# Attention with two mixture layers behind it: six of nine token blocks of the first layer moved behind the attention

## The chip, the core and the metric

The program runs on one core of a Trainium2 chip. The metric is the device time of one execution in microseconds; of the kernel before there are three runs, 1027.32, 1027.60 and 1028.91 us, median 1027.60. Names of engines: PE multiplies matrices (PEld loads its weights), DVE and ACT do elementwise work, POOL next to nothing here, SP issues the transfers.

## What is computed

Three layers in a row, in float32. B = 4, H = 8 heads, S = 576 positions, D = 64; 2304 tokens of 512 values; both feed-forward layers are 512 to 2048 to 512.

```python
scores = scale * np.matmul(q, k.transpose(0, 1, 3, 2))
scores = np.where(causal, -1000000000.0, scores)
a = np.exp(scores - scores.max(-1, keepdims=True))
a /= a.sum(-1, keepdims=True) + 1e-09
local = np.matmul(a, v)
q_p = phi(q)                                  # phi(x) = elu(x) + 1
mem_out = (q_p @ M_prev) / (q_p . z_prev + 1e-06)
attn = g * mem_out + (1 - g) * local          # g = sigmoid(beta)
x = attn as [2304, 512]
h = x @ w_in;  x = (h * sigmoid(h)) @ w_out   # "MoE 1"
h = x @ w2_in; x = elu(h) @ w2_out            # "MoE 2"
```

## The kernel before

**The planner.** The kernel's functions don't issue instructions. They record operations in a list (`Plan.add`), each with an engine, a cost and what it reads and writes. `Plan.schedule` (L301) then places them on the engines by a list scheduler with a cost model, forward and backward in turns, and `Plan.order` (L273) gives the sequence in which they are issued. So every engine works through a fixed queue, and all instructions carry the line of one helper, L192. A `boost` raises the rank of the first eight attention tasks, `nc.ahead(n)` that of what stands inside it.

**Attention** (`attention`, L963). A task is one pair of heads and a region of queries: "A" is queries 0 to 255, "B" 256 to 575, each with the keys up to its diagonal. Batch 0 has A and B as tasks of their own, the others one task for both, 20 tasks in all. `soft` (L762) makes the scores on PE, then on DVE the masked, negated scores with their minimum (`e<-s,mask`, in the trace CUSTOM_DVE_ANT_0), then on ACT the exponential with its row sum, on DVE the reciprocal of the sum times the gate (`sm<-sm,og`, RECIPROCAL), and the scaled weights, on ACT for the tiles "2", "3" and "4", on DVE for the "A" tiles. Each exponent tile `e` has one buffer per head and kind, so a task's minimum must wait until PE has transposed the task before (`a_T`, `b_T`: `tp<-ident,e`). `mem_soft` and `mem_T` make the memory term. `av_mm` and `av_end` (L890) multiply by the values; the last matmul of a region is `av<-pt,ms`, which closes it: 32 of these, called attention ends below. The result is copied to a tile `xt` and stored in `xdA`/`xdB`.

**Precision.** A float32 matrix is split into a high and a low part (`split2`, L428: a cast on ACT, a subtraction on DVE), and each product of two of them is three matmuls. The weights of MoE 1 and MoE 2 come as float64 and are taken apart by `w_value` (L488): a scaling on ACT, a TENSOR_SCALAR and two SCALAR_TENSOR_TENSOR on DVE for each tile; with `w_split` after it, ACT has two instructions for a tile and DVE four. 32 such tiles make MoE 1 (`w_stream`, L506), streamed beside the attention.

**MoE 1.** Nine token blocks of 256: (b, "A") and (b, "B") for four batches, and "T", the last 64 tokens of each batch. `moe1_block` (L560) does one block with 256 columns a matmul, 16 steps f of 12 matmuls for the first product (`h<-x,w`) and 12 for the second (`acc<-g,w`), that is 384 matmuls; between them ACT makes the tanh (`t<-h`), DVE `t<-t,h`, ACT and DVE the two parts of `g`. `moe1_wide` (L642) does two blocks together with 512 columns, 384 matmuls for both, with tiles in the pool `p2`, whose memory is that of the attention's pool `at`: nothing in `p2` may start before the last user of `at` is done. `first` (L1057) lists the blocks that go 256 wide beside the attention: 0A and 0B in two halves, then 1A, 1B and 2A (`LAST = 5`); `interleave` (L985) sets in which measure they are recorded between the attention's steps. Behind it come the wide pairs (3A, 3B) and (2B, T) (L1321, L1335).

**MoE 2** runs behind that, with its weights prepared from the second wide pair on.

Of the kernel before, what the change touches and what calls it, by code (L numbers as in the profile page):

```python
# [21 lines left out]
NORM = '234'  # L22
NATN = '234'
# [3 lines left out]
LAST = 5  # L27
# [3 lines left out]
PASSES = 4  # L31
COLD = 0.3735
NFILL = 70
LEND = 4
NAG = 1
LATE = 60
NAT1 = []
NAT2 = []
# [5 lines left out]

BOOST = 1000.0
# [107 lines left out]
class Plan:  # L153
# [147 lines left out]
    def schedule(self, back):  # L301
# [26 lines left out]
        for _ in ops:  # L328
# [5 lines left out]
            o = ops[heapq.heappop(ready[e])[1]]  # L334
# [26 lines left out]
def attention_moe_moe_kernel(  # L361
# [71 lines left out]
    mask = new(const, [128, 768], BF16, "mask")  # L433
# [9 lines left out]
    for p0, rows, c0, n in ((0, 128, 384, 128), (0, 64, 704, 64), (64, 64, 704, 64)):  # L443
# [26 lines left out]
    again = []  # L470

    whole = [(c, 2 * j + u) for c, js in ((0, NAT1), (1, NAT2)) for j in js for u in range(2)]

# [14 lines left out]
    def w_value(raw):  # L488
# [6 lines left out]
        nc.vector.scalar_tensor_tensor(out=raw[:, 0:512], in0=hi_w, scalar=3, in1=lo_w,  # L495
# [5 lines left out]
    def w_split(f, c, v):  # L501
        t = w_tile(f, c)
        split2(t[:, 512:1024], t[:, 0:512], v)
        (win, wout)[c][f] = t

    def w_stream(srcs, ahead, place, whole=(), last=2 * NF):  # L506
        todo = [(f, c) for f in range(NF) for c in range(2)]
        raws = {}

        def fetch(k):  # L510
            if k < len(todo) and k not in raws:
                f, c = todo[k]
                raws[k] = w_load(srcs[c], f, c, w_tile(f, c, I32) if (c, f) in whole else place(k))
# [4 lines left out]
        for k, (f, c) in enumerate(todo):  # L518
            fetch(k)
            raw = raws.pop(k)  # L520
            w_value(raw)
            if (c, f) in whole:
                (win, wout)[c][f] = raw
            else:
                w_split(f, c, f32(raw[:, 0:512]))
            if k + ahead < last:
                fetch(k + ahead)
            yield

    def w_again(c, f):  # L530

        v = new(mp, [128, 512], F32, "t", 2)
        nc.scalar.copy(v[:], f32((win, wout)[c][f][:, 0:512]))
        w_split(f, c, v[:])
# [25 lines left out]
    def moe1_block(blk, half, xraw, wnext=None, mid=None):  # L560
        j0, j1 = {None: (0, NF // 2), 0: (0, JH), 1: (JH, NF // 2)}[half]
        nat = (NAT1, NAT2) if half is not None else ((), ())
# [12 lines left out]
        def gemm1(j):  # L575
            for _ in range(NAG):
                if again:
                    w_again(*again.pop(0))
            hb = bank("h", 1)
            h = hb[:].rearrange("p (a n) -> p a n", a=2)  # L580
            if j not in nat[0] and not xt:
                x_split()
            for u in range(2):
                w = win[2 * j + u]
                n = 0
                for kt in range(4):
                    c = slice(kt * 128, (kt + 1) * 128)
                    if j in nat[0]:
                        mm(h[:, u, :], f32(w[:, c]), xraw[:, kt, :], kt == 0, kt == 3)
                        yield  # L590
                        continue
# [5 lines left out]
            g = None if j in nat[1] else new(mp, [128, 2, 2, 256], F32R, "g", 2)  # L597
            g_t[j] = g or t
            with nc.ahead(HP):
                nc.scalar.activation(t[:], h, AF.Tanh, scale=0.5)  # L600
                nc.vector.scalar_tensor_tensor(out=t[:], in0=t[:], scalar=1.0, in1=h, op0=ALU.add, op1=ALU.mult)
                if g:
                    split(g, t[:])

        def gemm2(j):
            g = g_t.pop(j)
            for u in range(2):
                w = wout[2 * j + u]
                for dm in range(4):
# [3 lines left out]
                    if j in nat[1]:  # L613
                        mm(acc[dm // 2][:, dm % 2, :], f32(w[:, c]), g[:, u, :], s0, last)
                        yield
                        continue
# [76 lines left out]
    bet = new(at, [128, H], F32, "sm40", 2)  # L693
    gg = new(at, [128, H], F32, "sm230", 2)
# [15 lines left out]
    def load(task):  # L710
# [14 lines left out]
        z = new(at, [128, 128], F32, "zb", 2)  # L725
# [36 lines left out]
    def soft(task, nms):  # L762
# [3 lines left out]
        tiles = [[], []]  # L766
        heads = range(1 if nms == "4" else 2)
        small = [new(at, [128, 8], F32, f"sm{nms}{u}", 2) for u in heads]
        for nm in nms:
            e = [new(at, [128, wide[nm]], F32, f"e{nm}{u}") for u in heads]  # L770
            for u in heads:
                e_t[task, u, nm] = e[u]
            if nm == "4":
                for i in range(2):
                    s = bank("s", 2)
                    c, n = ((0, 320), (320, 256))[i]
                    scores(task, [s[0:64, 0:n], s[64:128, 0:n]], 512, 576, c, c + n)
                    masked(e[0][:, c:c + n], s[:, 0:n], (0, 512)[i], 3e38 if i == 0 else small[0][:, 0:1],
                           small[0][:, i:i + 1])
                tiles[0].append((e[0], 0, 576, 1))  # L780
                continue
            s = [bank("s", 2), bank(f"acc{p % 2}") if rg == "A" else bank("s", 2)]
            parts = [(0, 0, 128), (1, 128, 256)] if nm == "A" else [(int(nm), 0, wide[nm])]
            for qt, off, n in parts:
                scores(task, [s[u][:, off:off + n] for u in heads], qt * 128, qt * 128 + 128, 0, n)
            for u in heads:
                for qt, off, n in parts:
                    c = len(tiles[u])
                    masked(e[u][:, off:off + n], s[u][:, off:off + n], 512 - n, 3e38, small[u][:, c:c + 1])
                    tiles[u].append((e[u], off, n, c))  # L790
        for u in heads:
            sm = small[u]
            for i, (e, off, n, c) in enumerate(tiles[u]):
                nc.scalar.activation(e[:, off:off + n], e[:, off:off + n], AF.Exp, scale=-1.0,
                                     bias=sm[:, c:c + 1], accum_out=sm[:, 2 + i:3 + i])
            k = len(tiles[u])
            r = sm[:, 4:4 + k]
            h = 2 * p + u
            nc.vector.tensor_scalar(out=r, in0=sm[:, 2:2 + k], scalar1=1e-9,
                                    scalar2=op[:, p:p + 1] if nms == "4" else og[:, h:h + 1], op0=ALU.add, op1=ALU.mult)  # L800
            nc.vector.reciprocal(out=r, in_=r)
            for i, (e, off, n, c) in enumerate(tiles[u]):
# [615 lines left out]
```

## Time and profile before

| | |
|---|---|
| runs | 1027.32, 1027.60, 1028.91 us |
| profiled execution | 1026.67 us, of it the span from first to last instruction 1024.5 us |
| PE busy | 1007.5 us (98%), 6534 matmuls |
| PEld busy | 848.9 us (83%) |
| DVE busy | 686.3 us (67%) |
| ACT busy | 599.4 us (59%) |
| transfers | 98.00 MB, mean 96 GB/s |
| granted TensorE clock, mean | 0.997 |

The page shows the busy share in 40 slices of 25.6 us as well: PE is at 7 tenths in the first two slices and at 9 or more behind them, DVE and ACT are high in the first seven and lower afterwards. A busy share is a mean over stages that have different limits, so the rows below are cut by stage. PE's busy time is that of overlapping, modelled spans (a 256-column matmul is shown as some 280 ns long and the next one starts 120 ns after it), so that the price of a matmul is read from start to start. The 2.2 us between 1024.5 and 1026.67 lie outside the instructions.

### The profile page before, as it was taken

What the parts mean: (1) busy time and instruction counts of PE and PEld (TensorE: products, weight loads), DVE (VectorE), ACT (ScalarE), POOL (GpSimd) and SP (SyncE); (2) the same over time, 40 slices, a digit from 0 to 9 for tenths busy, and PEclk for the clock granted to TensorE, in tenths of its full rate; (3) what the DMA queues carried; (4) which work ended last, traced back from release to release, by engine and by line L of the source; (5) the groups of instructions that cost most, each with busy time, mean ns of one, the idle gap of its engine ahead of it and who ended that gap; (6) DMA issues with size and microseconds to landing.
All of it is one profiled execution on the core that took longest, in us unless ns stands there. A gap on an engine that the chain in (4) does not pass through costs nothing.

```text
span 1024.5 us, 17493 instructions
## 1 busy us (share of the span) xinstructions
PE 1007.5 (98%) x6534; PEld 848.9 (83%) x6534; DVE 686.3 (67%) x1734; ACT 599.4 (59%) x1374; POOL 6.2 (1%) x30
## 2 busy tenths in 40 slices
PE   7799999999999999999999999999999999999998
PEld 5366877778777779998888888999899998989987
DVE  7999998656556553622223587969679975656554
ACT  6899998767667764423224455656567554444433
POOL 1000000000000000000000000000000000000000
PEclk9899999999999999999999999999999999999999
DMA  8655844333222212301003135323226130302010
GB/s 254 215 182 171 251 147 146 95 94 101 76 64 81 88 38 84 101 1 42 1 1 96 47 125 164 93 93 124 83 83 201 47 124 1 123 1 93 11 62 21
DMA packets 96724, 98.00 MB, mean 96 GB/s; under 512 B 10880, under 2 KB 82048, under 8 KB 96640
## 3 DMA queue, kind: packets, MB, share of 16 engines
q1 hardware_dynamic: 96640, 96.89, 30.3%
q8 instruction: 51, 0.84, 0.3%
q14 instruction: 33, 0.27, 0.1%
HBM read 76.94 MB, written 19.92 MB: 95 GB/s over the span
## 4 chain that ended last, share of the span: by engine, by line
PE 94%; DVE 2%; ACT 2%; DMA 1%; issue 0%; SPq 0%; DVEq 0%; ACTq 0%
PE acc L192 26%; PE s L192 19%; PE h L192 18%; PE tp L192 17%; PE av L192 13%; ACT e L192 1%; DVE w L192 1%; DMA raw<-in_moe_w_in 0%; DVE e L192 0%; SPq L192 0%; DVE eA L192 0%; DMA k<-in_kT 0%; ACT a L192 0%; ACT w L192 0%; ACT eA L192 0%
## 5 line engine op out<-in xcount | busy, mean ns | idle before, releaser
L192 PE MATMUL acc<-g,w 128*128 128x256 f32 (+1 forms) x1152 | 194.2, 310 | 0.0
L192 PEld LDWEIGHTS acc<-g,w 128*128 128x128 f32 x1152 | 161.5, 190 | 18.2 <-issue 9.2
L192 PE MATMUL s<-x,w 128*128 128x256 f32 (+1 forms) x1056 | 173.7, 302 | 0.0
L192 PEld LDWEIGHTS s<-x,w 128*128 128x128 f32 x1056 | 155.6, 190 | 14.1
L192 PE MATMUL h<-x,w 128*128 128x256 f32 x960 | 142.6, 293 | 0.1
L192 PE MATMUL tp<-x,w 128*128 128x256 f32 (+1 forms) x864 | 141.2, 306 | 0.0
L192 PEld LDWEIGHTS h<-x,w 128*128 128x128 f32 x960 | 124.2, 190 | 11.3 <-issue 8.7
L192 PEld LDWEIGHTS tp<-x,w 128*128 128x128 f32 x864 | 124.2, 190 | 9.6
L192 PE MATMUL acc<-w,g 128*128 128x512 f32 x480 | 127.9, 392 | 0.0
L192 ACT ACTIVATE e<-e,sm 128x384 f32<-128x384 f32 (+2 forms) x160 | 104.8, 687 | 7.3 <-DVE sm L192 7.2
L192 PEld LDWEIGHTS acc<-w,g 128*128 128x128 f32 x480 | 86.4, 189 | 14.4
L192 ACT COPY a<-tp 128x384 f32<-128x384 f32 (+2 forms) x160 | 64.2, 425 | 35.2 <-PE tp L192 30.3
L192 DVE SCALAR_TENSOR_TENSOR w<-w 128x512 int32<-128x512 int32 x116 | 78.3, 687 | 1.7 <-ACT w L192 0.4
L192 PE MATMUL s<-k,q 64*128 64x384 f32 (+5 forms) x368 | 71.0, 465 | 5.1 <-DMA k<-in_kT 3.1
L192 DVE CUSTOM_DVE_ANT_0 e<-s,mask 128x384 f32<-128x384 f32 (+2 forms) x80 | 45.3, 594 | 31.3 <-PE tp L192 29.9
L192 ACT CAST g<-e 128x512 fp32r<-128x512 f32 (+1 forms) x80 | 46.0, 578 | 34.1 <-DVE e L192 33.9
L192 DVE TENSOR_TENSOR g<-t,g 128x512 fp32r<-128x512 f32 x72 | 49.6, 688 | 23.6 <-ACT g L192 23.4
L192 ACT ACTIVATE e<-h 128x512 f32<-128x512 f32 (+1 forms) x80 | 47.0, 590 | 31.4 <-DVE h L192 30.6
L192 DVE TENSOR_TENSOR g<-e,g 128x512 fp32r<-128x512 f32 (+1 forms) x80 | 50.6, 635 | 21.6 <-ACT g L192 20.5
L192 PE MATMUL tp<-ident,e 128*128 128x128 f32 (+1 forms) x304 | 59.8, 284 | 3.4 <-ACT e L192 1.9
L192 ACT CAST g<-t 128x512 fp32r<-128x512 f32 x72 | 44.8, 622 | 26.3 <-DVE t L192 25.3
L192 DVE SCALAR_TENSOR_TENSOR t<-t,h 128x512 f32<-128x512 f32 x40 | 27.4, 684 | 48.8 <-ACT t L192 48.7
(135 smaller groups left out, 1447.0 us busy)
## 6 DMA issues: line engine op xcount, KB each, us to landing
w<-in_moe_w_in SPq DMA_DIRECT2D x29, 512.0 KB, 4.7
w<-in_moe_w_out SPq DMA_DIRECT2D x29, 512.0 KB, 3.7
k<-in_kT SPq DMA_DIRECT2D x16, 288.0 KB, 4.4
y<-y SPq DMA_DIRECT2D x18, 256.0 KB, 2.5
qm<-in_qn SPq DMA_DIRECT2D x32, 128.0 KB, 2.3
vr<-in_vn SPq DMA_DIRECT2D x16, 256.0 KB, 4.3
q<-in_qT SPq DMA_DIRECT2D x12, 288.0 KB, 3.7
xdB<-xt SPq DMA_DIRECT2D x16, 160.0 KB, 3.1
```

What stands on the lines that cost most here:

```text
L192: r = getattr(issue, fn)(*[a.make() if isinstance(a, View) else a for a in args], **{k: v.make() if isinstance(v, View) else v for k, v in ...
```

## The change

- `LAST` 5 to 3: beside the attention only 0A and 0B (in halves) and 1A are done 256 wide. The other six blocks go in three wide pairs, in the order of `WORD`: (1B, 2A), (3A, 3B), (2B, T). `RATIO` 0.7 records less MoE between the attention's steps.
- `EDUP`: the exponent tiles "A" and "2" get two buffers. To make room, the z vector has one buffer instead of two, the two heads of a pair share one tile of small numbers, the mask is 704 instead of 768 wide (tile "4" is taken as 384 + 192 keys instead of 320 + 256), and the result is copied into the transposed memory tile `pt` (two buffers, `xt` is gone).
- `soft`: the exponentials of both heads come first, then one SCALAR_TENSOR_TENSOR and one RECIPROCAL for all row sums of the pair, where each head had its own.
- The planner: for DVE and ACT in the forward pass, if an operation that ranks higher by over `YM` becomes ready within `YA` of the chosen one's cost, the engine is kept idle until then and takes that one.
- `w_stream`: the last two weight tiles are fetched in a step of their own; switches that were off (`NAT1`, `NAT2`, `again`) are gone.

```diff
-LAST = 5
+LAST = 3
+WORD = [3, 4, 6, 7, 5, 8]
+RATIO = 0.7
+YIELD = ("DVE", "ACT")
+YA = 0.6
+YM = 1000.0
+EDUP = "A2"
...
-            o = ops[heapq.heappop(ready[e])[1]]
+            key, i = heapq.heappop(ready[e])
+            o = ops[i]
+            if e in YIELD and not back and wait[e]:
+                end = t + YA * o.cost
+                soon = min(((ops[j].prio - ops[j].boost, j, w) for w, j in wait[e] if w < end), default=None)
+                if soon and soon[0] < key - YM:
+                    heapq.heappush(ready[e], (key, i))
+                    o, t = ops[soon[1]], max(t, soon[2])
...
-        z = new(at, [128, 128], F32, "zb", 2)
+        z = new(at, [128, 128], F32, "zb")
...
-            e = [new(at, [128, wide[nm]], F32, f"e{nm}{u}") for u in heads]
+            e = [new(at, [128, wide[nm]], F32, f"e{nm}{u}", 2 if nm in EDUP else 1) for u in heads]
...
-                    c, n = ((0, 320), (320, 256))[i]
+                    c, n = ((0, 384), (384, 192))[i]
...
+        nc.vector.scalar_tensor_tensor(out=cols(su), in0=cols(su), scalar=1e-9,
+                                       in1=ogs.unsqueeze(2).to_broadcast([128, k, k]), op0=ALU.add, op1=ALU.mult)
+        nc.vector.reciprocal(out=mx[:, 0:k * k], in_=su[:, 0:k * k])
...
-        pt = new(at, [128, w], F32, "pt")
+        pt = new(at, [128, 320], F32, "pt", 2)
...
-        xt = new(at, [128, 320], F32, "xt")
+        xt = pt_t.pop((task, r))
...
-    rest = interleave(attention(n0, len(tasks), hook2), g, 1.0)
-    w_take(33, 33)
+    rest = interleave(attention(n0, len(tasks), hook2), g, RATIO)
+    w_take(34, 34)
...
+    WIDE = [order[x] for x in WORD]
...
-    moe1_wide(order[6:8], ("x25", "x26"))
+    for i in range(LAST, 7, 2):
+        moe1_wide(WIDE[i - LAST:i - LAST + 2], ("x25", "x26"))
...
-    moe1_wide([order[5], order[8]], wnext=wnext)
+    moe1_wide(WIDE[-2:], wnext=wnext)
```

What the planner makes of it is seen in the engines' queues. First DVE, early in the attention, ahead of the first scores of the second "B" task of batch 0 (the ISA row is the masked score; `w` tiles are MoE 1's weights). Before:

```order
L192 SCALAR_TENSOR_TENSOR w_14_1_410<-w_14_1_410 128x512
L192 SCALAR_TENSOR_TENSOR w_14_1_487<-w_14_1_487 128x512
L192 TENSOR_SCALAR nm_625<-nm_625 128x6
L192 SCALAR_TENSOR_TENSOR qm_564<-em_651,qm_564 128x384
L192 RECIPROCAL nm_625<-nm_625 128x6
L192 TENSOR_SCALAR ms_617<-mr_580,gp_185 64x64
L192 TENSOR_TENSOR qm_472<-qm_472,nm_625 128x384
L192 TENSOR_TENSOR w_1_0_665<-w_15_0_277,w_1_0_665 128x512
L192 TENSOR_TENSOR w_2_0_672<-w_14_1_410,w_2_0_672 128x512
L192 ISA e_1_693,sm_2_694<-s_611,mask_96 128x384
```

Now, at the same place:

```order
L194 SCALAR_TENSOR_TENSOR sm_1_510<-sm_1_510,op_268 128x1
L194 TENSOR_SCALAR ms_539<-mr_486,gp_273 64x64
L194 RECIPROCAL sm_1_510<-sm_1_510 128x1
L194 TENSOR_TENSOR w_0_0_517<-w_14_0_155,w_0_0_517 128x512
L194 SCALAR_TENSOR_TENSOR w_14_0_173<-w_14_0_173 128x512
L194 ISA e_1_568,sm_2_569<-s_535,mask_96 128x384
```

Weight work has moved behind the attention's: the tiles at work are w_0 and w_14, where they were w_1 and w_2.

Second PE, some 15 us of matmuls behind the last attention end. Before, the next block follows 256 wide:

```order
L192 MATMUL acc_7_4808<-g_5470,w_13_0_2172 128x256 x6
L192 MATMUL acc_7_4821<-g_5470,w_13_0_2172 128x256 x6
L192 MATMUL h_5562<-x_6_5511,w_0_0_346 128x256 x3
L192 MATMUL h_5562<-x_6_5518,w_0_0_346 128x256
L192 MATMUL acc_7_4808<-g_5555,w_14_7_2477 128x256 x2
```

Now the first wide pair does, with its x split (x_0_4906 and x_0_4917) in the memory that the attention has left:

```order
L194 MATMUL acc_6_4164<-g_4883,w_13_0_2594 128x256 x6
L194 MATMUL acc_6_4177<-g_4883,w_13_0_2594 128x256 x6
L194 MATMUL s_4965<-x_0_4906,w_0_0_517 128x512
L194 MATMUL acc_6_4164<-g_4954,w_14_7_2849 128x256 x2
L194 MATMUL acc_6_4177<-g_4954,w_14_7_2849 128x256 x2
L194 MATMUL s_4965<-x_0_4917,w_0_0_517 128x512
```

The wide pair came one block later before, and now follows the block at work. Third ACT at that place, which makes the x that PE's first wide matmul reads (x21 is the high part, x25 and x26 are the loads of the two blocks, x27 a weight tile of MoE 2). Before:

```order
L192 CAST g_30_5470<-t_30_5451 128x512
L192 ACTIVATE h2_0_5440<-h2_0_5440 128x512
L192 CAST x21_0_5497<-x25_0_5423 128x2x256
L192 CAST x23_0_5504<-x25_0_5423 128x2x256
L192 CAST x0_6_5511<-stg_11_4532 128x256
L192 CAST x1_6_5518<-stg_11_4532 128x256
```

Now:

```order
L194 CAST g_22_4883<-t_22_4862 128x512
L194 ACTIVATE x27_0_4849<-x27_0_4849 128x512
L194 CAST x21_0_4906<-x25_0_4832 128x2x256
L194 CAST x23_0_4913<-x25_0_4832 128x2x256
L194 ACTIVATE t_23_4931<-h_24_4893 128x512
L194 CAST x21_0_4906<-x26_0_4841 128x2x256
L194 CAST x23_0_4913<-x26_0_4841 128x2x256
```

The casts from x26 stand directly behind those from x25 and one tanh, where the next 256-wide block's casts stood.

## Rows read from the trace of the kernel before

**Rows 1.** The page, part 4: the chain that ended last, by engine.

```profile
PE 94%; DVE 2%; ACT 2%; DMA 1%; issue 0%; SPq 0%; DVEq 0%; ACTq 0%
```

**Rows 2.** Stretches: length, busy us (instructions) of PE, PEld, DVE, ACT, POOL, then clock.

```profile
0.00:25.00 25.00, 19.13 (x142) 14.11 (x143) 17.96 (x84) 16.25 (x49) 2.64 (x13) 1.00 0.84 253
25.00:71.60 46.60, 40.21 (x235) 23.87 (x235) 46.38 (x149) 43.52 (x110) 0.61 (x3) 0.93 0.63 194
71.60:234.50 162.90, 162.82 (x1216) 126.36 (x1214) 137.79 (x434) 136.84 (x352) 1.49 (x7) 1.00 0.49 152
234.50:399.50 165.00, 165.00 (x1249) 130.70 (x1245) 93.42 (x335) 113.83 (x302) 1.43 (x7) 1.00 0.23 70
```

**Rows 3.** Timeline of PE at the 6th, 18th and 32nd attention end: start, us.

```profile
71.62 0.70 PE L192 MATMUL av<-pt,ms 128*128 128x320 f32 x2
...
234.51 0.81 PE L192 MATMUL av<-pt,ms 128*128 128x320 f32 x2
...
399.48 0.81 PE L192 MATMUL av<-pt,ms 128*128 128x320 f32 x2
```

**Rows 4.** The chain piece by piece, 256 columns: start, us, piece.

```profile
403.40 2.88 PE h L192 x24
```

**Rows 5.** The chain piece by piece, 512 columns.

```profile
469.37 2.72 PE s L192 x12
```

**Rows 6.** Stretches, MoE 1's weights alone: busy PE, PEld, DVE, ACT (instructions).

```profile
0.00:71.60 71.60, 11.31 (x67) 9.05 (x67) 25.48 (x43) 13.16 (x21) 0.95 0.70 215
71.60:234.50 162.90, 99.34 (x658) 85.27 (x657) 47.12 (x79) 26.31 (x41) 1.00 0.49 152
234.50:399.50 165.00, 104.05 (x666) 87.67 (x666) 0.00 (x0) 0.00 (x0) 1.00 0.23 70
```

**Rows 7.** Groups of instructions by form: busy us, mean ns of one, idle before.

```profile
L192 DVE TENSOR_SCALAR sm<-sm,og 128x2 f32<-128x2 f32 x32 | 7.2, 226 | 2.2 <-ACT e L192 2.1
L192 DVE RECIPROCAL sm<-sm 128x2 f32<-128x2 f32 x32 | 5.2, 162 | 0.3
```

**Rows 8.** One stretch, the MoE steps' tiles t alone: busy DVE, ACT (instructions).

```profile
71.60:234.50 162.90, 19.10 (x28) 17.16 (x28) 1.00 0.49 152
```

**Rows 9.** Timeline of PE in the attention: start, us, matmuls.

```profile
300.61 1.33 PE L192 MATMUL h<-x,w 128*128 128x256 f32 x9
301.77 0.40 PE L192 MATMUL acc<-g,w 128*128 128x256 f32 x2
302.10 1.13 PE L192 MATMUL s<-k,q 64*128 64x512 f32 x4
...
303.39 0.27 PE L192 MATMUL tp<-ident,qm 128*128 128x128 f32 x1
303.42 0.36 PE L192 MATMUL acc<-g,w 128*128 128x256 f32 x1
303.62 0.27 PE L192 MATMUL tp<-ident,qm 128*128 128x128 f32 x1
```

**Rows 10.** Timeline of SP behind the last attention end.

```profile
402.79 0.37 SPq L192 DMA_DIRECT2D x<-xdA  x1
...
406.13 0.51 SPq L192 DMA_DIRECT2D x<-in_moe_w_out  x1
```

**Rows 11.** Timeline of ACT behind the last attention end.

```profile
406.31 0.60 ACT L192 ACTIVATE t<-h 128x512 f32<-128x512 f32 x1 [3.69 <-PE h L192]
...
409.00 0.70 ACT L192 ACTIVATE h<-h 128x512 f32<-128x512 f32 x1 [0.72 <-DMA h<-in_moe_w_out]
409.86 1.15 ACT L192 CAST x<-x 128x512 fp32r<-128x512 f32 x2 [0.16 <-DMA x<-xdA]
```

**Rows 12.** Waits of DVE, 71.6 to 399.5 us: us in total, times, longest.

```profile
DVE e L192 <- PE tp L192: 29.9, 19, 4.0
```

**Rows 13.** Busy time and clock of one stretch, columns as in the second group.

```profile
42.00:48.00 6.00, 5.27 (x20) 2.58 (x21) 5.94 (x17) 5.70 (x17) 0.00 (x0) 0.50 0.74 222
```

**Rows 14.** The page, part 6: transfers, KB each, us to landing.

```profile
k<-in_kT SPq DMA_DIRECT2D x16, 288.0 KB, 4.4
```

More of the change, by code (lines that the diff above doesn't have):

```diff
@@ L22 @@
 NORM = '234'
-NATN = '234'
 XHP = 1000
@@ L442, in attention_moe_moe_kernel @@
     nc.gpsimd.memset(mask[:], 0.0)
-    for p0, rows, c0, n in ((0, 128, 384, 128), (0, 64, 704, 64), (64, 64, 704, 64)):
+    for p0, rows, c0, n in ((0, 128, 384, 128), (0, 64, 640, 64), (64, 64, 640, 64)):
         tri = mask[p0:p0 + rows, c0:c0 + n]
@@ L502, in w_split, with w_stream @@
         t = w_tile(f, c)
-        split2(t[:, 512:1024], t[:, 0:512], v)
+        split2(t[:, 512:1024], t[:, 0:512], f32(v))
         (win, wout)[c][f] = t
-    def w_stream(srcs, ahead, place, whole=(), last=2 * NF):
+    def w_stream(srcs, ahead):
         todo = [(f, c) for f in range(NF) for c in range(2)]
+        n = len(todo)
         raws = {}
         def fetch(k):
-            if k < len(todo) and k not in raws:
+            if k < n:
                 f, c = todo[k]
-                raws[k] = w_load(srcs[c], f, c, w_tile(f, c, I32) if (c, f) in whole else place(k))
+                i = n - LEND + k % LEND if k < n - LEND else n - 2 + k % 2
+                raws[k] = w_load(srcs[c], f, c, w_tile(*todo[i], I32) if k < n - 2 else new(at, [128, 1024], I32, "raw"))
         for k in range(ahead):
@@ L518, in w_stream @@
         for k, (f, c) in enumerate(todo):
-            fetch(k)
             raw = raws.pop(k)
             w_value(raw)
[L522 to L526, printed above, removed]
+            w_split(f, c, raw[:, 0:512])
+            if k + ahead < n - 2:
                 fetch(k + ahead)
             yield
[L530 to L534, printed above, removed]
+            if k == n - 3:
+                fetch(n - 2)
+                fetch(n - 1)
+                yield
     def part(w, i):
@@ L575, in gemm1 @@
         def gemm1(j):
-            for _ in range(NAG):
-                if again:
-                    w_again(*again.pop(0))
             hb = bank("h", 1)
             h = hb[:].rearrange("p (a n) -> p a n", a=2)
-            if j not in nat[0] and not xt:
+            if not xt:
                 x_split()
@@ new lines, in soft, with cols @@
+                for qt, off, n, c in parts:
+                    c += 2 * u
+                    masked(e[u][:, off:off + n], s[u][:, off:off + n], 512 - n, 3e38, mx[:, c:c + 1])
+                    tiles.append((nm, e[u], off, n, c, mx[:, c:c + 1]))
+        for nm, e, off, n, c, m in tiles:
+            nc.scalar.activation(e[:, off:off + n], e[:, off:off + n], AF.Exp, scale=-1.0, bias=m,
+                                 accum_out=su[:, c:c + 1])
+        k = len(heads)
+        def cols(v):
+            return v[:, 0:k * k].rearrange("p (u t) -> p u t", u=k)
```

95 lines of the change are left out of this document (28 added, 67 removed).

## The prediction

> **What bounds the kernel now.** I read the chain of waits first: PE holds 94% of it [rows 1]. So PE's work in order sets the end, and a gain has to be less PE work, or less time in which PE has none. The busy time by stretch comes next [rows 2]. I cut it by "attention ends": the matmul av<-pt,ms closes one query region of one head pair, 32 times in all; the 6th starts at 71.6, the 18th at 234.5 (its row begins 234.51), the 32nd at 399.5 us [rows 3]. In 0 to 25 us PE has 19.13 us of work, in 25 to 71.6 it has 40.21 of 46.60, and there DVE is full: 46.38 us, with ACT at 43.52. From 71.6 on PE is full (162.82 of 162.90, then 165.00 of 165.00) while DVE falls from 137.79 to 93.42 and ACT from 136.84 to 113.83. So DVE sets the time up to the 6th end, and PE behind it. The last view is the chain piece by piece, which prices a matmul: 24 of 256 columns take 2.88 us, 0.120 each [rows 4]; 12 of 512 columns take 2.72 us, 0.227 each [rows 5].
>
> Counted in the two built programs, the 256-wide MoE matmuls ahead of the 6th, 18th and 32nd end were 67, 724 and 1390 (the trace has 67, 658 more and 666 more [rows 6]) and are now 34, 549 and 1004. Ahead of the 6th end DVE had 43 weight instructions [rows 6], now 29; ACT 22 (one of them starts after 71.6), now 16.
>
> **Width.** Blocks 1B and 2A leave the 256-wide path: 768 matmuls x 0.120 = 92.2 us go and 384 x 0.227 = 87.0 come, all on PE where it is full: -5.1 us.
>
> The rows put 2 x 0.120 = 0.240 us against 0.227, a gap of 13 ns for each pair. The Trainium skill, page "TensorE: Matmul & The Clock Gate", section "Back-to-back issue gap", has the gap of isolated matmuls as columns over 2.4 GHz plus 2.5 ns, which would be 109 and 216 ns and so a gap of 2.5 ns for each pair. By that rule the width would bring 1.0 us and the forecast would be 4.1 us later; both rows are of this kernel, are above it, and decide.
>
> **Up to the 6th end.** 14 weight instructions fewer on DVE, at the mean of the 43 (25.48 / 43 = 0.593 us [rows 6]): -8.3. The merged row sums save one TENSOR_SCALAR and one RECIPROCAL for each pair of heads (0.226 + 0.162 = 0.39 us [rows 7]); some six pairs here: -2.3. DVE alone would then reach the end at 71.6 - 10.6 = 61.0 us. ACT loses 6 weight instructions (13.16 / 21 = 0.627 us each: -3.8): it was busy 16.25 + 43.52 = 59.8 us of 71.6 [rows 2], so 56.0 are left, and with the 8.75 us in which it is idle in the first 25 it allows 64.7. I take **64.7**; 61.0 (ACT finds its work earlier) and 71.6 (no gain) are the ends. Of these 6.9 us, 33 MoE matmuls x 0.120 = 4.0 are only put off.
>
> **6th to 18th end.** MoE matmuls 658 to 515: 143 x 0.120 = -17.2 us. PE also changes over less often between runs of MoE and attention matmuls: 98 runs to 87. A run's price I bound by two pieces of the timeline [rows 9]: 9 + 2 matmuls from 300.61 to 302.10 take 1.49 us where 11 x 0.120 = 1.32, so 0.17 more; a single one between two transposes takes 303.39 to 303.62 with one of these, 0.23 us, no more than the two by themselves. Transposes are the commoner neighbour, so I take 0.05, with 0 and 0.17 as ends: -0.6. PE needs 162.9 - 17.8 = 145.1 us. Its feeders come close: DVE 137.8 + 8.3 (the weights put off) - 3 x 1.36 (three MoE steps fewer; 14 of them take 19.10 us [rows 8]) - 12 x 0.39 = 137.3 us, 95%; ACT 136.8 + 3.8 - 3 x 1.23 (17.16 / 14) = 136.9 us, 94%. Against 46.38 of 46.60 that DVE managed from 25 to 71.6 us [rows 2] that can be borne, but not quite without holes: +2 us, with 0 and 10 as ends. **147.1** us.
>
> **18th to 32nd end.** 666 to 455: 211 x 0.120 = -25.3; 123 runs to 64: -3.0. 165.0 - 28.3 = **136.7** us, with ACT at 113.8 - 4.4 x 1.23 = 108.4 us (79%) and DVE lower. The 32nd end comes at 64.7 + 147.1 + 136.7 = 348.5 us, 51.0 earlier.
>
> **Behind the attention.** 530 256-wide matmuls were left, now 148: -45.8; the new wide pair brings 384 x 0.227 = +87.0: +41.2 us. One place is new: PE has 124 matmuls, 14.9 us, between the last attention end and the first wide matmul, which waits for x21. What has to happen before it is in the rows of now, counted from 399.5: the loads into the freed memory go out at 402.8 to 406.1 (+3.3 to +6.6) [rows 10], the third load's first use is at 409.00 (+9.5), the first cast of x at 409.86 (+10.4) [rows 11]. In the new ACT queue stand a weight scaling (0.70), two casts (1.15), a tanh (0.60; its h is ready at 100 matmuls, +12.4) and the cast that PE waits for (0.6): about +13.6 against +15.3. Hidden by 1.7 us; every us more than that in the loads is a us at the end. I take 0, up to 3.
>
> **Nothing for the rest.** The second buffers of eA and e2 remove waits such as DVE's for PE's transposes (29.9 us in 19 waits [rows 12]), in stretches where DVE has time to spare; they are what lets DVE reach 95%, and without them the +2 above would be nearer its 10. The single z buffer puts a load behind the last reader; behind it on SP stand the next task's loads, which have a task's time, 165.0 / 7 = 23.6 us, where the page shows 4.4 us from issue to landing [rows 14]: 0, at most 3. Splitting the 576 keys as 384 + 192 instead of 320 + 256 changes no sum. "Engines wait" is the planner's rule; on the chip it is only an order.
>
> **The sum.** -51.0 + 41.2 = -9.8 us on the profiled execution's 1026.67: 1016.9. The median shown, 1027.6, is 0.9 above that execution, so I give **1017.8**.
>
> **Rivals.** (1) *Only the width counts*: attention loses as much beside it as before, since queues that are fuller make as many holes as the earlier start takes away. For it: 95 and 94%. Against: DVE's 99% from 25 to 71.6 us. 1026.67 - 5.1 = 1021.6, 1020 to 1025 with the hand-over's 3 us.
> (2) *DVE and ACT starve PE* between the 6th and the 18th end, because each waits for the other in a fixed order. If they stay at the share that DVE had there before (137.79 of 162.9, 84.6%), 137.3 us of work take 162.3 instead of 147.1: +15.2, so 1032.1, slower. It decides from the point where the stretch takes 156.9 us, that is below 88%. For it: DVE's waits for PE [rows 12]. Against: before, PE was full there, so DVE's low share was only lack of work.
> (3) *The clock stays low longer at the start.* Now the granted clock is 0.50, the 1.2 GHz level, from 42 to 48 us [rows 13], after 25 to 40 us of attention matmuls between idle pieces; the first MoE matmuls stood ahead of the 5th end, now all stand behind it. PE's work from 25 us to the 6th end is at most 40.21 - 3 (half of that 6 us) - 4.0 = 33.2 us of 39.7, so 6.5 us of loss are hidden; 20 us at the lower level would lose 10 and give 1020.4, and it takes 33 us for the whole gain to go. For it: the order ahead of the 5th end. Against: the filler matmuls are still there, and the lower level of now cost one short piece.
> (4) *More than I take*: DVE's 61.0 us, no holes, and runs at 0.17: down to 1003.
>
> **How the numbers follow.** The measurement can tell about 0.2% from no change, 2 us: 1025.5 to 1029.7 is "same". My forecast, 1010 to 1020, has 0.62; (1) 0.18; (4) 0.06; (2) 0.09, a third of it within the same; (3) 0.05, half of it faster, a quarter the same. So faster 0.88, same 0.05 (0.04 and what is at the edge of (1)), slower 0.07. The range leaves out (2) and the far part of (4): 1009 to 1026.
>
> **What would show it.** In the new profile: the 6th end near 65 us, with DVE and ACT full ahead of it; the 18th near 212 with PE full and DVE and ACT at 93 to 95%; the 32nd near 348; the first 512-wide matmul some 15 us later with no idle time ahead of it; 256 and 512 columns at 0.120 and 0.227. It is wrong if PE idles by over 6 us between the 6th and 18th end, if the clock is low for over 13 us, or if PE waits for x21.

## The result and the profile after

The change takes 1019.79 us (median of 1016.20, 1019.17, 1020.42 and 1020.43), before 1027.51: a ratio of 0.9915, 95% interval 0.9890 to 0.9940. The forecast was 1017.8 us with a range of 1009 to 1026. The profiled execution took 1019.17 us, its span 1017.2 (before 1026.67 and 1024.5).

The chain by engine, the row that answers to [rows 1], still belongs to PE:

```profile
PE 94%; DVE 3%; DMA 1%; ACT 1%; issue 0%; POOL 0%; DVEq 0%; POOLq 0%
```

The stretches, cut at the new attention ends, columns as in [rows 2]:

```profile
0.00:25.00 25.00, 18.73 (x154) 13.11 (x154) 17.56 (x89) 18.08 (x59) 2.54 (x13) 1.00 0.80 249
25.00:65.00 40.00, 34.85 (x195) 19.61 (x194) 36.24 (x108) 35.73 (x91) 0.61 (x3) 0.87 0.57 176
65.00:211.90 146.90, 146.39 (x1073) 109.14 (x1071) 137.97 (x417) 137.59 (x352) 1.60 (x7) 1.00 0.56 172
211.90:350.90 139.00, 139.00 (x1035) 103.47 (x1031) 84.99 (x301) 109.23 (x290) 1.43 (x7) 1.00 0.29 86
```

The timeline of PE at the 6th, 18th and 32nd attention end, as in [rows 3], and at the first 512-wide matmul:

```profile
64.99 0.70 PE L194 MATMUL av<-pt,ms 128*128 128x320 f32 x2
...
211.93 0.81 PE L194 MATMUL av<-pt,ms 128*128 128x320 f32 x2
...
350.91 0.81 PE L194 MATMUL av<-pt,ms 128*128 128x320 f32 x2
...
366.42 0.40 PE L194 MATMUL s<-x,w 128*128 128x512 f32 x1
```

| step, us | before | forecast | after |
|---|---|---|---|
| up to the 6th end | 71.6 | 64.7 | 65.0 |
| 6th to 18th | 162.9 | 147.1 | 146.9 |
| 18th to 32nd | 165.0 | 136.7 | 139.0 |
| 32nd end to the end of the span | 625.0 | 666.2 | 666.3 |
| span | 1024.5 | 1014.7 | 1017.2 |

(625.0 is 1024.5 - 399.5, and 666.3 is 1017.2 - 350.9.) From 65.0 us on PE is full: it lacks 0.5 us in the second stretch and nothing in the third, with DVE at 137.97 of 146.90 us (94%) and ACT at 137.59. The weights alone, columns as in [rows 6], confirm the counts of matmuls from the built program, 34 and 455; the row between shows 517 where the program has 515, two of them across the cut:

```profile
0.00:65.00 65.00, 6.56 (x34) 5.20 (x34) 19.13 (x32) 10.26 (x16) 0.92 0.66 204
65.00:211.90 146.90, 82.48 (x517) 67.20 (x515) 54.28 (x90) 29.26 (x46) 1.00 0.56 172
211.90:350.90 139.00, 69.94 (x455) 58.59 (x455) 0.00 (x0) 0.00 (x0) 1.00 0.29 86
```

The prices of [rows 4, 5] are unchanged in the chain of after, 0.120 and 0.227 us for a matmul:

```profile
355.06 2.88 PE h L194 x24
...
374.94 2.72 PE s L194 x12
```

The hand-over on SP and ACT, where [rows 10, 11] stood:

```profile
354.16 0.37 SPq L194 DMA_DIRECT2D x<-xdB  x1
```

```profile
360.57 0.71 ACT L194 ACTIVATE x<-x 128x512 f32<-128x512 f32 x1 [0.62 <-DMA x<-in_moe_w_out]
361.26 1.14 ACT L194 CAST x<-x 128x512 fp32r<-128x512 f32 x2
363.80 0.60 ACT L194 ACTIVATE t<-h 128x512 f32<-128x512 f32 x1 [1.39 <-PE h L194]
364.29 1.13 ACT L194 CAST x<-x 128x512 fp32r<-128x512 f32 x2
```

The first load goes out 3.25 us behind the 32nd end; the second block's high part is the first of the two casts at 364.29, so it is ready at about 364.9 (+14.0; +13.6 was forecast), and PE's first wide matmul starts at +15.5 without waiting. DVE's wait for PE's transposes, [rows 12], has gone from 29.9 us in 19 waits to 18.9 in 10 between the 6th and the 32nd end:

```profile
DVE e L194 <- PE tp L194: 18.9, 10, 4.6
```

What differs from the forecast in kind is the clock. Three stretches of after, columns as in [rows 2]:

```profile
40.00:45.00 5.00, 3.57 (x18) 1.63 (x17) 4.92 (x16) 4.69 (x13) 0.00 (x0) 0.89 0.77 251
45.00:50.00 5.00, 5.00 (x21) 2.44 (x18) 4.00 (x15) 3.15 (x7) 0.20 (x1) 0.50 1.00 341
50.00:55.00 5.00, 5.00 (x22) 3.18 (x21) 2.79 (x8) 3.69 (x10) 0.00 (x0) 0.59 0.26 82
```

A mean of 0.89, 0.50 and 0.59 over 5 us each is 5 x (0.11 + 0.50 + 0.41) / 0.5 = 10.2 us at the 1.2 GHz level (before, one piece of 6.8 us). From 45 us on PE is full in it, and DVE and ACT, full around it, fall to between 2.79 and 4.00 of 5 us: here PE holds them up.

The clock column shows no low value before PE has first reached the upper level, so the start of the program has to be read from the matmuls. One score matmul of before follows the other by 0.38 us at 8.2 us, and by 0.21 us at 15.7 us:

```profile
8.21 0.58 PE L192 MATMUL s<-k,q 64*128 64x128 f32 x1 [1.11 <-DMA k<-in_kT]
...
8.59 0.42 PE L192 MATMUL s<-k,q 64*128 64x128 f32 x1
...
15.65 0.37 PE L192 MATMUL s<-k,q 64*128 64x128 f32 x1 [0.78 <-DMA k<-in_kT]
...
15.86 0.27 PE L192 MATMUL s<-k,q 64*128 64x128 f32 x1
```

The change is at full pace from 6.55 us on (its rows stand under "No fillers" below). The first clock record of the trace is at 14.4 us before and at 6.3 us now, so before has some 8 us more at the lower level at its start. The fillers, bf16 matmuls at the start whose result nothing reads, all run in the first 12 us of the change; before, 40 of the 70 do. The prediction saw only the piece from 42 to 48 us. What these 8 us are worth is in no term of its sum, and no run tells it apart from the other early gains.

### The profile page after: what moved, and what is told of

Read it like the earlier page. It is cut to its first block, busy times and chain, and to the rows that moved or that the text cites. A ratio compares the mean times of both kernels' runs of the same rounds, so it can differ in the third digit from the quotient of the medians.

```text
span 1017.2 us, 16692 instructions
## 1 busy us (share of the span) xinstructions
PE 1000.5 (98%) x6150; PEld 825.5 (81%) x6150; DVE 685.6 (67%) x1666; ACT 603.0 (59%) x1370; POOL 6.2 (1%) x30
## 4 chain that ended last, share of the span: by engine, by line
PE 94%; DVE 3%; DMA 1%; ACT 1%; issue 0%; POOL 0%; DVEq 0%; POOLq 0%
PE acc L194 24%; PE s L194 22%; PE tp L194 19%; PE h L194 15%; PE av L194 14%; DVE w L194 1%; DMA w<-in_moe_w_in 1%; DVE e L194 1%; DMA zb<-in_z_prev 1%; DVE eA L194 1%; DVE nm L194 0%; DVE qm L194 0%; DVE em L194 0%; ACT w L194 0%; ACT a L194 0%
## 5 line engine op out<-in xcount | busy, mean ns | idle before, releaser
L194 PE MATMUL s<-x,w 128*128 128x256 f32 (+1 forms) x1152 | 197.5, 309 | 0.0
L194 PEld LDWEIGHTS s<-x,w 128*128 128x128 f32 x1152 | 173.5, 190 | 17.3
L194 PE MATMUL tp<-x,w 128*128 128x256 f32 (+1 forms) x960 | 164.3, 314 | 0.0
L194 PE MATMUL acc<-g,w 128*128 128x256 f32 (+1 forms) x864 | 160.8, 325 | 0.0
L194 PEld LDWEIGHTS tp<-x,w 128*128 128x128 f32 x960 | 143.0, 190 | 13.9
L194 PEld LDWEIGHTS acc<-g,w 128*128 128x128 f32 x864 | 128.7, 190 | 18.1 <-issue 6.4
L194 PEld LDWEIGHTS acc<-w,g 128*128 128x128 f32 x480 | 86.5, 189 | 14.3
L194 PE MATMUL h<-x,w 128*128 128x256 f32 x576 | 95.5, 299 | 0.5 <-ACT w L194 0.5
L194 PEld LDWEIGHTS h<-x,w 128*128 128x128 f32 x576 | 76.8, 191 | 11.9 <-issue 9.8
L194 ACT COPY a<-tp 128x384 f32<-128x384 f32 (+2 forms) x160 | 64.1, 424 | 26.7 <-PE tp L194 15.7
L194 DVE CUSTOM_DVE_ANT_0 e<-s,mask 128x384 f32<-128x384 f32 (+1 forms) x80 | 46.6, 606 | 26.1 <-PE tp L194 18.9
L194 PE MATMUL av<-w,g 128*128 128x512 f32 x192 | 58.0, 392 | 0.0
```

The lines of the kernel that those rows point to most:

```text
L194: r = getattr(issue, fn)(*[a.make() if isinstance(a, View) else a for a in args], **{k: v.make() if isinstance(v, View) else v for k, v in ...
```

## The experiments

The runs were made in four sets, the change and then e1 to e4, e5 to e8 and e9 to e12, each beside runs of before. The columns: median of the runs; ratio to before with its 95% interval; then from the profiled execution the three attention ends and, in brackets, the 256-wide MoE matmuls ahead of each.

| run | us | ratio | 6th, 18th, 32nd end |
|---|---|---|---|
| before (medians of the sets) | 1027.5 to 1028.4 | 1 | 71.6 (67), 234.5 (724), 399.5 (1390) |
| the change | 1019.79 | 0.9915 [0.9890, 0.9940] | 65.0 (34), 211.9 (549), 350.9 (1004) |
| e1_width_alone | 1020.76 | 0.9932 [0.9919, 0.9944] | 71.7 (59), 207.1 (496), 350.1 (984) |
| e2_narrow | 1025.92 | 0.9974 [0.9964, 0.9984] | 66.9 (34), 236.8 (741), 399.6 (1390) |
| e3_one_buffer | 1023.88 | 0.9966 [0.9953, 0.9979] | 71.6 (46), 214.4 (535), 353.1 (984) |
| e4_no_yield | 1019.48 | 0.9913 [0.9900, 0.9926] | 67.4 (44), 205.7 (498), 348.6 (983) |
| e5_ratio1 | 1021.87 | 0.9933 [0.9921, 0.9945] | 67.0 (34), 235.5 (741), 359.0 (1049) |
| e6_fill140 | 1018.24 | 0.9906 [0.9892, 0.9920] | 61.4 (24), 216.7 (600), 352.3 (1031) |
| e7_one_buffer_z2 | 1023.34 | 0.9953 [0.9941, 0.9966] | 72.9 (48), 217.6 (528), 355.2 (984) |
| e8_word | 1016.83 | 0.9892 [0.9877, 0.9907] | 63.7 (34), 209.6 (549), 348.6 (1004) |
| e9_again | 1017.29 | 0.9889 [0.9874, 0.9903] | 62.3 (34), 208.1 (549), 347.1 (1004) |
| e10_no_fill | 1023.79 | 0.9953 [0.9940, 0.9967] | 68.9 (24), 217.8 (549), 356.8 (1004) |
| e11_only_2 | 1022.53 | 0.9942 [0.9930, 0.9955] | 71.2 (61), 209.2 (504), 351.7 (984) |
| e12_word_fill140 | 1018.33 | 0.9900 [0.9887, 0.9914] | 62.2 (24), 217.5 (600), 353.0 (1031) |

One reading serves all of them: take 0.120 us for each MoE matmul off a stretch, and the rest is what the attention takes. Between the 18th and the 32nd end it is 165.0 - 666 x 0.12 = 85.1 us before, 84.4 in the change, and 82.8 to 86.6 in every run; between the 6th and the 18th 82.9 to 87.1. PE is full there, to within 2 us, in all of them. Up to the 6th end it is 58.2 to 67.2, and there the runs part.

**Width alone.** The kernel before, with the wide pairs of the change:

```diff
-LAST = 5
+LAST = 3
+WORD = [3, 4, 6, 7, 5, 8]
+RATIO = 0.7
...
-    rest = interleave(attention(n0, len(tasks), hook2), g, 1.0)
+    rest = interleave(attention(n0, len(tasks), hook2), g, RATIO)
...
-    moe1_wide(order[6:8], ("x25", "x26"))
+    WIDE = [order[x] for x in WORD]
+    for i in range(LAST, 7, 2):
+        moe1_wide(WIDE[i - LAST:i - LAST + 2], ("x25", "x26"))
...
-    moe1_wide([order[5], order[8]], wnext=wnext)
+    moe1_wide(WIDE[-2:], wnext=wnext)
```

> The kernel before with one part of the change: LAST, WORD and RATIO, so that six blocks go in wide pairs; one buffer for each exponent tile, a row sum for each head and the planner's old rule stay. My theory: the width is worth 5.1 us by itself, so about 1022.4 us against 1027.5; the 6th attention end stays near 71 us (44 weight instructions of DVE ahead of it, as before) and 256-wide matmuls ahead of the 32nd end are 984. Rival (the new buffers and sums carry the change): without them DVE and ACT starve PE once there is less filling beside the attention, the stretch from the 6th to the 18th end shows PE idle by over 6 us, and the time is 1026 us or more.

Measured: 1020.76, 7.3 us below before's 1028.06 in the same set of runs; between the profiled executions it is 5.6 (span 1018.9 against 1024.5, the clock low for equally long, at the start too). The working of 5.1 stands; the 1.0 us that the prediction gives for isolated matmuls lies outside the interval (5.8 to 8.3 us). No starving without the second buffers either: from the 6th end to the 32nd PE is busy in every us:

```profile
71.70:207.10 135.40, 135.40 (x997) 99.89 (x996) 126.13 (x417) 129.66 (x339) 1.43 (x7) 1.00 0.57 173
207.10:350.10 143.00, 143.00 (x1067) 109.12 (x1066) 90.38 (x335) 111.23 (x297) 1.43 (x7) 1.00 0.29 85
```

**Everything but the width.**

```diff
-LAST = 3
-WORD = [3, 4, 6, 7, 5, 8]
-RATIO = 0.7
+LAST = 5
+WORD = [6, 7, 5, 8]
+RATIO = 1.0
```

> The change without its width: LAST = 5 and RATIO = 1.0 again, five blocks 256 wide beside the attention and two wide pairs behind it; buffers, sums and the planner's rule as changed. My theory: what is left is the early part, 2.9 us, and a few changeovers less (211 runs instead of 236), so 1024 to 1025 us, with the 6th end at 65 us as in the changed kernel and the 32nd near 393. Rival (the buffers and the order carry the change): 1019 to 1021 us.

Measured: 2.1 us below before (1025.92 against 1028.06), just above the theory's range and far from the rival's, with the 6th end at 66.9. Between the profiled executions there is nothing (span 1024.6 against 1024.5). The parts give 7.3 + 2.1 = 9.4, and the change has 7.7 in its first set of runs and 11.0 in its second.

**One buffer for each exponent tile.**

```diff
-EDUP = "A2"
+EDUP = ""
```

> The change with one buffer for every exponent tile (EDUP empty). My theory said that the second buffers let DVE reach 95% between the 6th and 18th end and that without them the holes there grow from 2 towards 10 us: 1021 to 1028 us, with DVE waiting for tp there. Rival (DVE has time to spare, the buffers are worth nothing): 1018 to 1021 us. DVE has 38 weight instructions ahead of the 6th end here instead of 29, so by the early part alone that end should come near 69 us.

Measured: 1023.88, 4.1 above the change's first median and 6.6 above its second. The place isn't the one that the prediction had in mind. Stretches of this run, then the weights alone in the first of them:

```profile
71.60:214.40 142.80, 142.80 (x1050) 106.39 (x1048) 132.44 (x405) 134.53 (x346) 1.44 (x7) 1.00 0.55 168
```

```profile
0.00:71.60 71.60, 7.15 (x46) 6.07 (x46) 23.43 (x41) 12.90 (x20) 0.95 0.68 209
```

Behind the 6th end PE is full, and the attention's rest is 142.8 - 489 x 0.12 = 84.1 us, no worse than the change's 85.1. Ahead of it DVE has 41 weight instructions where the change has 32, 4.3 us more (23.43 - 19.13), and the end comes at 71.6. So most of what the second buffers do here they do through the order: with a free buffer the next attention task can be placed ahead of weights. Weights are not all of it. DVE's first instruction is another one here and waits longer than the change's (first row: this run, second: the change):

```profile
DVE og L194 <- ACT og L194: 6.8, 1, 6.8
...
DVE qm L194 <- ACT qm L194: 4.8, 1, 4.8
```

DVE's waits for PE's transposes, which the prediction named, don't show ahead of the 6th end in this run.

**The planner's rule.**

```diff
-YIELD = ("DVE", "ACT")
+YIELD = ()
```

> The change with the planner's old rule (no engine kept idle for a higher rank), so the same instructions in another order; 35 weight instructions of DVE ahead of the 6th end instead of 29. My theory: the rule is worth what it moves off DVE's queue there, 6 x 0.593 = 3.6 us at the 6th end, of which some 1 to 2 us remain at the end: 1020 to 1023 us. Rival (the order within the queues does not matter where PE is full): 1018 to 1020 us.

Measured: 1019.48, the change's time. The rule is worth nothing here that can be told in this set of runs; the rival holds.

**The measure of MoE between the attention's steps.**

```diff
-RATIO = 0.7
+RATIO = 1.0
```

> The change with RATIO back at 1.0: the same work, recorded in another measure between the attention's steps. In the built program 741 MoE matmuls stand ahead of the 18th attention end (549 in the change) and 1049 ahead of the 32nd (1004), in 267 runs ahead of the 32nd (159). By the prediction's price of 0.05 us for a changeover between MoE and attention matmuls it is 108 x 0.05 = 5.4 us slower than the change, about 1025. By the theory that I have now (the stretch from the 18th to the 32nd end took 139.0 us where 211 matmuls fewer alone give 139.7, so a changeover costs next to nothing) it is the same within 2 us: 1018 to 1022. A third way: with more MoE ahead of the 18th end PE never runs out there, and it is up to 2 us faster.

Measured: 1021.87, at the upper edge of the second theory, well below the first. But this run doesn't test the price of a changeover: its trace has 8, 88 and 67 runs of MoE matmuls in the three stretches, 163 ahead of the 32nd end and not 267, where the change has 8, 87 and 64. The last stretch, with 308 MoE matmuls in 67 runs:

```profile
235.50:359.00 123.50, 123.50 (x888) 86.56 (x886) 77.56 (x286) 102.21 (x277) 1.43 (x7) 1.00 0.27 81
```

Its rest is 123.5 - 308 x 0.12 = 86.5 us, where the change has 84.4 with 64 runs; in the stretch ahead of it the rest is 83.6 against 85.1, so over both it is 0.7 us more. Of the 2.9 us between the spans (1020.1 against 1017.2) 2.0 stand at the 6th end already, and why is not shown. What a changeover costs is seen from other runs: before, with 123 runs in the last stretch, gives (85.1 - 84.4) / 59 = 0.01 us, and the width alone, with 107 runs, has a rest of 84.4, the change's.

**More fillers.**

```diff
-NFILL = 70
+NFILL = 140
```

> The change with 140 filler matmuls at the start instead of 70; in the built program the last of them stand ahead of the 5th attention end. The change has one piece of 10.24 us at the lower clock ahead of the 6th end. Theory: that piece costs little, since DVE and ACT set the pace up to the 6th end, so that the time stays within 2 us of the change, 1018 to 1021, whether or not the piece goes. Rival 1: the piece costs half its length, the fillers keep the clock up, and the kernel is 3 to 5 us faster, 1015 to 1017. Rival 2: the fillers (30 take 3.4 us, so 70 more take 7.9 us, in about 10 us of idle time) stand in front of attention work, and it is 3 us or more slower, over 1022.

Measured: 1018.24, in the theory's range. The 6th end is early (61.4) with 10 MoE matmuls fewer ahead of it; nothing is gained by the end of the program that the repeat of the change below doesn't have too.

**One exponent buffer, two for z.** Beside `EDUP = ""`:

```diff
-        z = new(at, [128, 128], F32, "zb")
+        z = new(at, [128, 128], F32, "zb", 2)
```

> The change without the second exponent buffers and with two buffers for z again: what is left of the change beside the attention is the merged row sums, the shared tiles and the split at 384 keys. The run without second exponent buffers took 1023.9. Theory: z is not what cost there (its load has a task's time), so it is the same, 1022.5 to 1025.5. Rival: the single z buffer makes DVE wait for the load early on (2.6 us in three waits in that run, and 0.5% of the span in the chain of the change), so it is 2 to 3 us faster than that run, 1020.5 to 1022.

Measured: 1023.34, as without it. The single z buffer costs nothing that shows.

**Another order of the wide pairs.**

```diff
-WORD = [3, 4, 6, 7, 5, 8]
+WORD = [6, 7, 3, 4, 5, 8]
```

> The change with the wide pairs in another order: (3A, 3B) first, then (1B, 2A), then (2B, T). The first pair now needs what the last attention tasks store, so that its loads can't start before the last store has landed (issued 1.35 us behind the last attention end, some 2.6 us to landing, against 3.25 us at which the first load goes out in the change). The cast that PE's first wide matmul reads ended at about 365.4 us in the change, 1.0 us ahead of that matmul. Theory: the store delays the first load by about 0.7 us and PE waits for 0 to 2 us: 1019 to 1022. Rival: the loads' landing behind the stores is later by 5 us or more, and each us shows at the end: 1024 or more.

Measured: 1016.83. PE waits for nothing; its first wide matmul starts at 364.06, again 15.5 us behind the 32nd end (348.55). The last store and the first loads:

```profile
349.90 0.32 SPq L194 DMA_DIRECT2D xdB<-pt  x1
351.81 0.37 SPq L194 DMA_DIRECT2D x<-xdA  x1
352.24 0.86 SPq L194 DMA_DIRECT2D x<-xdB  x1
```

The first load is 3.26 us behind the end, as in the change. SP waits for the last store to land before it, and does so in the change as well, where the first load reads another block (first row: this run, second: the change):

```profile
SPq L194 <- DMA xdB<-pt: 1.2, 1, 1.2
...
SPq L194 <- DMA xdB<-pt: 1.2, 1, 1.2
```

So this order adds no wait, and neither expectation explains a time that is 3 us lower. But all engines' queues are the same as the change's up to the 32nd end, so this is a second sample of one order, and its clock was low for less: 0.34 x 5 / 0.5 = 3.4 us, in one piece.

```profile
15.00:20.00 5.00, 4.66 (x27) 2.69 (x28) 4.25 (x19) 3.14 (x12) 0.00 (x0) 0.66 0.92 299
```

**The change once more,** with no edit.

> The change itself once more, beside the three runs below. The run with the wide pairs in another order has the same instructions in the same order on every engine up to the 32nd attention end, and its profile shows 3.41 us at the lower clock and the 32nd end at 348.6 us, where the change's first profile shows 10.24 us and 350.9. Theory: the two are one kernel up to there, and what differs is how long the clock was low, at about a third of a us for each us; the median is then 1016.5 to 1020.0, and among its own runs those with a higher mean clock are the shorter ones. Rival: the order of the pairs is itself worth 3 us, and the median stays at 1019.5 to 1020.5.

Measured: 1017.29 (1015.38, 1017.06, 1017.52, 1018.23). The profiled execution is the shortest, 1015.38 us with a span of 1013.4, and shows no low piece:

```profile
core 0: 1013.4 us, clock 1.000
```

```profile
62.28 0.70 PE L194 MATMUL av<-pt,ms 128*128 128x320 f32 x2
...
208.13 0.81 PE L194 MATMUL av<-pt,ms 128*128 128x320 f32 x2
...
347.12 0.81 PE L194 MATMUL av<-pt,ms 128*128 128x320 f32 x2
```

```profile
0.00:62.30 62.30, 49.32 (x347) 30.50 (x348) 53.52 (x196) 53.68 (x149) 3.15 (x16) 1.00 0.70 212
62.30:208.10 145.80, 145.80 (x1073) 109.04 (x1071) 137.71 (x418) 137.51 (x352) 1.60 (x7) 1.00 0.57 173
```

With the same queues, pieces of 10.2, 3.4 and 0 us at the lower clock go with spans of 1017.2, 1014.9 and 1013.4 us. The theory holds in the main, but not all of the difference is the clock's. The 4th attention end stands ahead of the low piece of the change's first profile, which begins at 43.9 us (first row: that profile, second: the repeat):

```profile
33.86 0.60 PE L194 MATMUL av<-pt,ms 128*128 128x256 f32 x2
...
34.21 0.60 PE L194 MATMUL av<-pt,ms 128*128 128x256 f32 x2
```

There the first profile is 0.35 us ahead, and at the 6th end it is 2.71 behind (64.99 against 62.28): 3.1 us for 10.2, 0.30 each. The other 1.1 us up to the 18th end come later, 0.5 of them where PE waits for a weight tile at 88.16 us. The run with the other order of pairs is 1.43 us behind the repeat at the 32nd end, but 0.79 of that ahead of its low piece, which begins at 15.9 us: PE waits longer for a load (first row: that run, second: the repeat).

```profile
15.34 0.34 PE L194 MATMUL s<-k,q 64*128 64x128 f32 x1 [2.53 <-DMA k<-in_kT]
...
14.55 0.34 PE L194 MATMUL s<-k,q 64*128 64x128 f32 x1 [1.43 <-DMA k<-in_kT]
```

So the landing of transfers differs between executions too. That a higher mean clock goes with a shorter run is only a tendency: among these four the one at 0.995 took 1017.06, the one at 0.997 took 1017.52. Over the 13 executions of these queues (the change's two sets and the other order of pairs) a straight line through span and mean clock gives 0.28 us for each us at the lower level.

**No fillers.** These matmuls add nothing to the result.

```diff
-NFILL = 70
+NFILL = 0
```

> The change without the filler matmuls at the start (they add nothing to the result). PE's first 40 us are then attention matmuls between idle pieces alone. Theory: the clock is at the lower level for some 20 us or more ahead of the 6th end, and by the third of a us for each us that the two runs above show, that is 3 to 6 us more than in the change: 1020 to 1025. Rival 1: it costs nothing, as DVE and ACT set the pace there: 1018 to 1020. Rival 2: each us at the lower level costs half a us, and it stays low for 30 us or more: over 1026.

Measured: 1023.79, 6.5 above the change of the same set of runs (1017.29). Its clock column shows little, as it has no low value before PE first reaches the upper level. The start to start of one score matmul does. First this run, then the change:

```profile
20.38 0.55 PE L194 MATMUL s<-k,q 64*128 64x128 f32 x1 [0.44 <-DMA k<-in_kT]
...
20.73 0.42 PE L194 MATMUL s<-k,q 64*128 64x128 f32 x1
```

```profile
4.85 0.58 PE L194 MATMUL s<-k,q 64*128 64x128 f32 x1
...
5.23 0.42 PE L194 MATMUL s<-k,q 64*128 64x128 f32 x1
...
6.55 0.34 PE L194 MATMUL s<-k,q 64*128 64x128 f32 x1
...
6.74 0.27 PE L194 MATMUL s<-k,q 64*128 64x128 f32 x1
```

0.38 us at the start and 0.19 from 6.55 on in the change, still 0.35 at 20.4 us without fillers (from 28 us on its scores are at full pace). That is some 20 us at the start and a piece of 3.4 us later (0.87 and 0.79 over 30 to 40 us), 23 to 24 us more than in the repeat, for 9.7 us of span (1023.1 against 1013.4): 0.4 for each us, if all of it is the clock's. That is not shown, since without the fillers the planner's order is another one: 37 of DVE's weight instructions and 24 MoE matmuls ahead of the 6th end, where the change has 32 and 34. That end is at 68.9 against 62.3.

**Second buffers for "2" alone.**

```diff
-EDUP = "A2"
+EDUP = "2"
```

> The change with second buffers for the exponent tiles "2" alone, not for "A". Without either it took 1023.9 and 1023.3. In the built program 61 MoE matmuls and 39 of DVE's weight instructions stand ahead of the 6th attention end (34 and 29 in the change, 46 and 38 with no second buffers). Theory: what the second buffers bring is that attention comes ahead of the weights up to the 6th end, at 0.593 us for each of DVE's weight instructions, so that with 39 of them the 6th end is at 71 us or later and the time is as without second buffers, 1022.5 to 1025. Rival: it is the wait of the "2" tiles' scores for PE's transposes that costs, all through the attention, and the time is that of the change, 1018 to 1021.

Measured: 1022.53, at the lower edge of the theory, and the 6th end at 71.2. The early tasks are those of batch 0, where "A" is a task of its own, so it seems that the second "A" buffers are needed for the early gain; "A" alone was not run. DVE's first wait is 6.8 us here too.

**Both edits that had the lowest times.**

```diff
-WORD = [3, 4, 6, 7, 5, 8]
+WORD = [6, 7, 3, 4, 5, 8]
...
-NFILL = 70
+NFILL = 140
```

> The change with the wide pairs in the order (3A, 3B), (1B, 2A), (2B, T) and with 140 fillers, the two edits that ran at 1016.8 and 1018.2 alone. If both count, 1015 to 1016.5. If what they show is one and the same, fewer us at the lower clock, it is 1016 to 1018.5, no better than the fillers alone. If the clock is at the lower level for 3.5 us or less in the profile and the 6th end comes by 62 us, as with the fillers alone, the fillers did it.

Measured: 1018.33, no better than either. No version beats the change by more than its own runs differ.

## Why the prediction came out, step by step

**The method held:** PE's order sets the end, and counting its matmuls by stretch gave the time within 2 us (1019.79, and 1017.29 in the repeat, for 1017.8). That it came so near is in part luck: the repeat's profile is 2.4 us earlier than forecast at the 6th end, 1.3 us shorter up to the 18th and 2.3 us longer up to the 32nd. Behind the 32nd end the working was exact: +41.2 forecast, +41.3 measured. The hand-over's cost of 0 was right, and so was its order of events (+13.6 and +15.3 forecast, +14.0 and +15.5 found); e8 shows that it stands with the wide pairs in another order.

**Width, -5.1:** e1 has -5.6 between profiled executions and -7.3 [5.8, 8.3] between medians (its interval times 1028.06). The Trainium skill, page "TensorE: Matmul & The Clock Gate", section "Back-to-back issue gap", would have it at -1.0 by its gap for isolated matmuls; both prices of this kernel are 11 ns above that rule (0.120 against 0.109, 0.227 against 0.216), and as a wide pair has half as many matmuls, that surcharge is what is saved. Of the six blocks in wide pairs four stood behind the attention before as well; the term is that of the two that moved, 1B and 2A.

**Up to the 6th end, 64.7:** measured 65.0, but as two errors that cancel. The repeat, without a low piece, got to 62.3 us: ACT is idle for 8.6 us up to there, about the 8.75 that I took as a floor, but has 53.68 us of work and not the 56.0 that I had worked out. The first profile is 2.7 us later, with its low piece. DVE's sum came out, 64.3 - 10.6 = 53.7 us and 53.80 measured (17.56 + 36.24), but again as two errors: the trace has 32 weight instructions by then and not 29, so the weights are 6.4 us less (25.48 - 19.13) and not 8.3, and the rest of DVE's work 4.2 us less and not 2.3.

**6th to 18th, 145.1 + 2 = 147.1:** measured 146.9. The repeat needs 145.8 with PE busy throughout, so DVE and ACT at 94% make next to no holes. The 0.5 us that PE lacks in the first profile are one wait for a weight tile.

**18th to 32nd, 136.7: the term that was mis-sized.** I took 0.05 us for each run of MoE matmuls, 3.0 us in all. The stretch lost 26.0 us where 211 x 0.12 = 25.3 are matmuls, so 0.7 for 59 runs, 0.01 each. The bound of 0 was nearer. That is 2.3 us of the 2.5 by which the span (1017.2) lies above the forecast (1014.7).

**Second buffers at nothing:** wrong in place. Without them the change loses 4 to 7 us (e3, e7), not as holes behind the 6th end but ahead of it, for the most part through weights that come first. I had their effect in the sum all the same, since the 14 weight instructions fewer (11 in the trace) were counted in the built program. How much the merged row sums bring by themselves stays open: e3, which has them, reaches the 6th end no earlier than e1, which doesn't, with 13 MoE matmuls fewer ahead of it, and ends 3 us later; that edit was not run alone.

**z, split, planner's rule at nothing:** z and the rule confirmed by e7 and e4; the split was not tried alone.

**The rivals.** (1) holds for the larger part: the width alone has 7.3 of the 7.7 us of the change's first set and of the 11.0 of its second, and brings the 32nd end as far forward (350.1). What speaks against it are the 2.1 us that e2 has without the width, and that the repeat's interval (0.9874 to 0.9903) lies below e1's (0.9919 to 0.9944); part of that may be e1's start, which is at the lower level as long as before's. (2) fell: PE lacked 0.5 us between the 6th and 18th end. (3) was part of the truth: the clock was low for 10.2 us in one piece, and the 6.5 us that I held to be hidden were not, since PE is the one that the others wait for in such a piece. It cost 0.3 us for each us, 3.1 in the first profile; the repeat's profile has no such piece. Against (3) I held that before had one short piece at the lower level; its first 14 us are at the lower level too. (4) fell, with changeovers at 0.01.

## What to carry to other kernels

Count the bounding engine's instructions per stretch from the built order, price them by start to start, and leave small prices (a changeover) at the end of their bounds that the commonest row shows. Before a difference of 2 or 3 us is given to an edit, compare how long the clock was low in both profiles, and run the unchanged kernel again beside it. Look at the waits for transfers as well, since their landing differs between executions. A second buffer may act not by removing a wait but by letting the planner put other work first: look at what stands ahead of the first stages.

## What the runs showed of the hardware that was not expected

Executions of one order differ by up to 5 us (1015.38 to 1020.43 for the change, over two sets of runs). Three profiles of the same queues had pieces of 10.2 and 3.4 us and none at 1.2 GHz between 15 and 55 us, both after attention matmuls between idle pieces. The Trainium skill, page "TensorE: Matmul & The Clock Gate", section "What's actually happening", says that the number of matmuls at the lower level at a kernel's start varies from run to run of one kernel; these traces show such a difference later, and nearly the same start (the first clock record at 5.7 to 6.3 us). What decides it in a given run is not shown here. The same page, section "Terms", prices the time at the lower level at about half its length; here the piece of 10.2 us cost 0.30 us for each us, and 13 executions give 0.28. Why it is less than half is not shown. And the clock column can read 1.00 where PE runs at half pace: in the change up to 6.5 us, before up to some 14 us and without fillers up to some 26 us, told by the start to start alone.
